# Guess of the experts by bf16 matmuls on upper halves, gate sums on GpSimd: one change to an attention and mixture-of-experts kernel

## The chip, the cores and the metric

The kernel runs on one core of a Trainium2 chip. The metric is the device time of one execution in microseconds. The time before is 491.83 us, the median of three runs (489.59 to 491.87).

## What is computed

Multi-query attention over 8 batches, 16 heads, 384 positions and 64 values a head, and behind it a mixture of experts with a gate in two levels (4 groups of 4 experts). Cut to what matters:

```python
def _attn_ref(q, k, v):                      # q (8,16,384,64), k and v (8,1,384,64)
    scores = np.matmul(q, k.transpose(0, 1, 3, 2)) / np.sqrt(64)
    attn = softmax(scores)
    return np.matmul(attn, v)
x = attn_out.transpose(0, 2, 1, 3).reshape(3072, 1024)
def _moe_ref(x, w_group, w_expert, w1, w2):  # w1, w2: (4,4,1024,1024)
    g_idx = np.argmax(x @ w_group, axis=1)
    for g in range(4):
        xg = x[g_idx == g]
        e_idx = np.argmax(xg @ w_expert[g], axis=1)
        for e in range(4):                   # tokens of xg with e_idx == e
            out[tokens] = gate_weight * (np.maximum(xg_e @ w1[g, e], 0) @ w2[g, e])
```

All tensors are float32. The attention weights are close to even, so a token's `x` is close to the mean of `v` over its batch, and nearly all tokens of a batch choose the same expert.

## The kernel before

**Rounds.** The attention is cut into 192 units (8 batches, 3 row tiles, 8 pairs of heads). The loop at line 1264 takes two units in each of 96 rounds, 12 rounds for each batch. A round has these steps: TensorE (PE) computes the scores of both units into two PSUM buffers `s` (L297, later L283); VectorE (DVE) takes the row maxima (L314); ScalarE (ACT) computes the exponentials with their sums (L319); DVE transposes the probabilities of the round two before into `ring` (L385); DVE takes the reciprocal of the sums (L330); GpSimd (POOL) multiplies by it (`norm`, L334). In some rounds PE multiplies the transposed probabilities with the values (`pv`, L416, 96 matmuls), and ACT copies the result (L427). Queries are transposed on PE (L244) and copied by ACT (L248) in the first five row tiles, later on DVE. Four units of the first batch go another way (`whole`, `pv_whole`, L347, L348, L356).

**Order by hand.** Each engine runs its instructions in the order in which the program writes them. `at(slot, where, fn)` files a step under a round and a place in it, and the loop calls the places in the order "s", "b", then "m0", "m1", "m3" (not in rounds with `pv`), "v", "m2", the first transpose, "t", the second transpose, "w", the norm, "e", "o", "g". So "w" lies ahead of a round's norm on POOL and behind its transposes on DVE, "v" ahead of the transposes, and "e" behind the norm. The norm of rounds 0, 2 and 3 comes one round later (`LATE`). Lines 1202 to 1214 file the steps of the guess.

**The guess.** The kernel has to begin the load of an expert's weights (2 tensors, 1024 x 1024) long before the tokens of a batch are known, so it guesses the expert of each batch from the mean of `v`:

- `guess_load` (L548) takes a weight buffer (`w1`) as scratch, names its parts and loads all rows of `v` into it by three DMAs of SP's queue;
- `guess_fold` (L565, POOL) builds a 128 x 128 matrix of zeros and ones from the identity, which folds the 16 heads of the gate's weights together; it also clears `spread` and makes `sixteen`;
- `guess_gate` (L576, PE) sums the gate weights `wge` (8 chunks of 128 rows, 32 columns) over the heads by eight float32 matmuls with `fold`; ACT copies the result to `gate` (L583);
- `guess_mean` (L585, PE) sums `v` over positions by 12 float32 matmuls with one column; ACT copies `mean` (L594);
- `guess_spread` (L596, POOL) multiplies `gate` by `mean` in two instructions (L600);
- `guess_logits` (L606, PE) sums over the partitions by one float32 matmul (L608); ACT copies `L` (L611);
- `guess_top`, `guess_first` (DVE, L615, L620), `guess_score` (POOL, L628 and L633), `guess_best` (DVE, L639), `guess_pick` (POOL, L644) find the expert of each batch, and `guess_picked` (L652) its mark.

The profile counts each float32 matmul of this kind as two passes. `load_main(0, 0)` reads the pick and issues the first weights on POOL's queue (L746). A matmul on `ident` (`busy`, L129) stands behind `guess_logits`.

**Logits of the first row tile.** `logits(0, 0, 1)` (L449, 16 matmuls) and DVE's copy of its result (`logits_out`, L465) stand in rounds 8 and 9. Their PSUM bank, as those of L244, L347, L356, L416 and all steps of the guess, is one of four that are handed out in turn.

**Main stage and end.** From round 17 on the matmuls of the guessed expert (L799, L784) are put between those of the attention. Tokens whose expert was not guessed are treated at the end; a loop (line 1406) runs once for each batch and expert that is left over.

Of the kernel before, what the change touches and what calls it, by code (L numbers as in the profile page):

```python
# [10 lines left out]
BF16 = mybir.dt.bfloat16  # L11
I32 = mybir.dt.int32
P = 128
# [6 lines left out]
def kernel(  # L20
# [527 lines left out]
    def guess_load():  # L548
# [4 lines left out]
        for name, w in (  # L553
            ("rows", B * ST * D), ("fold", P), ("gate", 32), ("mean", B // 2), ("spread", B * NL), ("L", B * NL),
            ("top", B * NL // 4), ("first", B * NL), ("score", B * GE), ("best", B), ("sixteen", GE),
        ):
            parts[name] = rows[:, at_:at_ + w]
            at_ += w
        for j in range(ST):
            nc.sync.dma_start(  # L560
                out=parts["rows"][:, j * B * D:(j + 1) * B * D].rearrange("p (b d) -> p b d", b=B),
                in_=v[:, 0, j * P:(j + 1) * P, :].rearrange("b p d -> p b d"),
            )

    def guess_fold():  # L565
        g = st["guess"]
        nc.gpsimd.tensor_tensor(
            out=g["fold"].rearrange("p (h d) -> p h d", h=2), in0=ident[:, 0:D].unsqueeze(1).to_broadcast([P, 2, D]),
            in1=ident[:, D:P].unsqueeze(1).to_broadcast([P, 2, D]), op=ALU.add,
        )  # L570
        nc.gpsimd.memset(g["spread"], 0.0)
# [3 lines left out]

    def guess_gate():  # L576
        g, bank = st["guess"], xbank()
        for ko in range(KO):
            nc.tensor.matmul(  # L579
                out=bank[:, 0:32], lhsT=g["fold"], rhs=wge[:, ko, :],  # L580
                start=(ko == 0), stop=(ko == KO - 1),
            )
        nc.scalar.copy(out=g["gate"], in_=bank[:, 0:32])  # L583

    def guess_mean():  # L585
        g, bank = st["guess"], xbank()
        rows = g["rows"].rearrange("p (j i x) -> p j i x", j=ST, x=P)
        for i in range(B // 2):
            for j in range(ST):
                nc.tensor.matmul(  # L590
                    out=bank[:, i:i + 1], lhsT=rows[:, j, i, :], rhs=w4[:, 0, 3:4],
# [4 lines left out]
    def guess_spread():  # L596
        g = st["guess"]
        for h in range(2):
            rows = slice(h * D, (h + 1) * D)
            nc.gpsimd.tensor_tensor(  # L600
                out=g["spread"][rows].rearrange("p (i h e) -> p i h e", h=2, e=NL)[:, :, h, :],
# [4 lines left out]
    def guess_logits():  # L606
        g, bank = st["guess"], xbank()
        nc.tensor.matmul(  # L608
            out=bank[:, 0:B * NL], lhsT=w4[:, 0, 3:4].to_broadcast([P, P]), rhs=g["spread"], start=True, stop=True
# [529 lines left out]
    for b in range(B):  # L1139
# [5 lines left out]
        if early:  # L1145
            at(x, "m2" if edge else "m0", logits, b, 0, 1)
            at(x + edge, "v", logits_out, b, 0, 1)
# [53 lines left out]

    at(3, "g", guess_load)
    at(4, "e", guess_fold)
    at(5, "m3", guess_gate)
    at(8, "m3", guess_mean)
    at(8, "e", guess_spread)
# [3 lines left out]
    at(10, "e", guess_score)  # L1210
    at(11, "v", guess_best)
    at(11, "e", guess_pick)
# [245 lines left out]
```

## Time and profile before

| what | value |
|---|---|
| median of three runs | 491.83 us (489.59, 491.87, 491.83) |
| the profiled execution | 488.88 us |
| its span, first to last instruction | 487.3 us |
| mean granted TensorE clock | 0.988 |
| PE busy | 471.9 us (97%) |
| DVE busy | 402.6 us (83%) |
| ACT busy | 321.0 us (66%) |
| POOL busy | 295.1 us (61%) |

Rows of the timeline hold the start in us, the duration in us, the engine, the line and the operation, the output and inputs by name, their shape, the number of instructions merged into the row and, in brackets, how long the engine stood idle before and what ended that. A row that merges several instructions gives the sum of their time; rows of one engine may overlap a little, since matmuls are pipelined. PEld is the weight load of TensorE. Rows of stretches hold the stretch, its length, the busy time of PE, PEld, DVE, ACT and POOL with the number of instructions, the granted TensorE clock as a share of full speed, the busy share of the DMA engines, and GB/s.

### The profile page before, as it was taken

How to read it: one execution, taken by the hardware profiler on the slowest of the kernel's cores; microseconds unless marked ns; L12 is line 12 of the kernel's file. 1: busy time of each engine (PE TensorE's matmuls, PEld its weight loads, DVE VectorE, ACT ScalarE, POOL GpSimd, SP SyncE). 2: the span in 40 equal slices, each digit the busy share in tenths (PEclk: the TensorE clock that was granted, in tenths of full speed). 3: DMA queues.
4: the chain of work that ended last, by engine and by line, in shares of the span. 5: the costliest groups of instructions: out<-in, count | busy, mean ns of one | idle time of the engine just before them, and what ended most of it. 6: DMA issues, size and time to landing. Idle time of an engine off the chain costs nothing.

```text
span 487.3 us, 21461 instructions
## 1 busy us (share of the span) xinstructions
PE 471.9 (97%) x8935; PEld 284.9 (58%) x8945; DVE 402.6 (83%) x707; ACT 321.0 (66%) x988; POOL 295.1 (61%) x536
## 2 busy tenths in 40 slices
PE   7799898999999999999999999999999999999997
PEld 3366555655665565655666566656665566655554
DVE  4948898998998989898999989898999988883352
ACT  5837675777685866677585767687585867672431
POOL 2836687566656667566656557566757657585223
PEclk9979998999999999999999999999999999999999
DMA  5553079789696969799596968789596947679993
GB/s 135 92 125 77 3 144 239 184 183 193 157 211 180 203 140 191 192 186 205 151 210 176 198 151 179 196 186 207 135 226 176 207 102 145 175 126 212 240 238 144
DMA packets 66291, 83.08 MB, mean 171 GB/s; under 512 B 25447, under 2 KB 42635, under 8 KB 65936
## 3 DMA queue, kind: packets, MB, share of 16 engines
q0 software_dynamic: 18736, 39.32, 44.5%
q1 hardware_dynamic: 46368, 42.03, 32.1%
q8 instruction: 72, 1.18, 0.9%
q10 hardware_dynamic: 1088, 0.33, 0.3%
q14 instruction: 27, 0.22, 0.1%
HBM read 99.94 MB, written 18.22 MB: 242 GB/s over the span
## 4 chain that ended last, share of the span: by engine, by line
PE 89%; DVE 4%; ACT 2%; POOL 2%; issue 1%; DMA 1%; SPq 0%; POOLq 0%; DVEq 0%
PE x L416 24%; PE x L799 22%; PE s L297 17%; PE s L283 7%; PE x L784 7%; PE sb L784 6%; PE x L455 2%; ACT pr L319 2%; DVE ring L385 2%; DVE nmx L314 2%; POOL pr L334 2%; PE x L579 1%; PE x L590 1%; DMA q_sb<-in_q_dram 1%; PE x L1080 0%
## 5 line engine op out<-in xcount | busy, mean ns | idle before, releaser
L334 POOL TENSOR_SCALAR pr<-pr,rinv 128x384 f32<-128x384 f32 x384 | 218.2, 587 | 141.6 <-DVE rinv L330 139.2
L319 ACT ACTIVATE pr<-s,nmx 128x384 f32<-128x384 f32 x384 | 218.4, 579 | 118.2 <-DVE nmx L314 97.3
L314 DVE TENSOR_REDUCE nmx<-s 128x2 f32<-128x768 f32 (+1 forms) x221 | 176.7, 845 | 44.6 <-PE s L297 27.4
L385 DVE STREAM_TRANSPOSE ring<-pr 128x768 f32<-128x768 f32 x189 | 174.7, 953 | 0.0
L416 PE MATMUL x<-ring,v_sb 32*64 32x384 f32 (+3 forms) x3264 | 131.1, 459 | 0.5 <-issue 0.5
L297 PE MATMUL s<-kt,qt 64*64 64x384 f32 x1120 | 107.7, 495 | 5.7 <-ACT pr L319 4.8
L416 PEld LDWEIGHTS x<-ring,v_sb 32*64 32x64 f32 x3264 | 85.3, 132 | 40.8 <-issue 3.4
L319 ACT ACTIVATION_READ_ACCUMULATOR pr<-s,nmx 128x1 f32 x384 | 77.5, 202 | 0.0
L297 PEld LDWEIGHTS s<-kt,qt 64*64 64x64 f32 x1120 | 37.9, 134 | 49.0 <-ACT pr L319 29.7
L799 PE MATMUL x<-xb,w 64*64 64x384 bf16 x1344 | 62.4, 328 | 0.0
L799 PE MATMUL x<-w,h_t 64*64 64x512 bf16 (+1 forms) x1152 | 57.1, 340 | 0.0
L799 PEld LDWEIGHTS <-w 64*64 64x64 bf16 x1344 | 42.6, 108 | 21.0 <-issue 9.6
L799 PEld LDWEIGHTS <-h_t 64*64 64x64 bf16 x1152 | 34.1, 107 | 24.2 <-issue 9.0
L283 PE MATMUL s<-kt,qt 32*64 32x384 f32 x832 | 40.7, 488 | 0.0
L427 ACT COPY xt<-x 128x384 f32<-128x384 f32 (+3 forms) x68 | 26.1, 470 | 12.9 <-PE x L416 12.9
L746 POOL DMA_DIRECT2D w<-in_moe_w_dram x36 | 27.8, 772 | 7.0 <-PE x L416 3.6
L283 PEld LDWEIGHTS s<-kt,qt 32*64 32x64 f32 x832 | 21.4, 131 | 12.2 <-issue 2.7
L826 ACT ACTIVATE h_t<-x 128x384 bf16<-128x384 f32 x56 | 24.5, 498 | 0.2
L784 PEld LDWEIGHTS <-w 128*128 128x128 bf16 x176 | 15.9, 98 | 15.0 <-issue 5.7
L868 ACT ACTIVATE y<-x,gsel 128x512 f32<-128x512 f32 (+1 forms) x43 | 24.5, 639 | 0.0
L784 PEld LDWEIGHTS <-h_t 128*128 128x128 bf16 x152 | 13.8, 97 | 16.0 <-issue 2.5
L784 PE MATMUL x<-xb,w 128*128 128x384 bf16 x112 | 20.6, 327 | 0.0
(176 smaller groups left out, 278.9 us busy)
## 6 DMA issues: line engine op xcount, KB each, us to landing
w<-in_moe_w_dram POOLq DMA_DIRECT2D x36, 1024.0 KB, 11.4
out_dram<-y SPq DMA_DIRECT2D x84, 128.0 KB, 3.3
q_sb<-in_q_dram SPq DMA_DIRECT2D x52, 112.0 KB, 5.8
xb_scratch<-xb SPq DMA_DIRECT2D x7, 768.0 KB, 9.8
q_sb<-in_q_dram SPq DMA_DIRECT2D x24, 224.0 KB, 4.3
q_sb<-in_q_dram SPq DMA_DIRECT2D x52, 64.0 KB, 8.7
v_sb<-in_v_dram SPq DMA_DIRECT2D x32, 96.0 KB, 3.3
kk<-in_k_dram SPq DMA_DIRECT2D x28, 92.0 KB, 3.1
```

The costliest lines, as they stand in the source:

```text
L283: last = nc.tensor.matmul(out=st["s", us[g // 2]][m * D:(m + 1) * D, g % 2, 0:S], lhsT=q4[r, (g + n) % 2, ts(m, D)], rhs=kt[r, :], start=( ...
L297: nc.tensor.matmul(out=s[m * D:(m + 1) * D, h, 0:S], lhsT=qt[r, ts(2 * cc + m, D)], rhs=kt[r, :], start=True, stop=True, tile_position=(h ...
L314: top = nc.vector.tensor_reduce(out=nmx[:, hs], in_=s[:, hs, 0:S], axis=AX.X, op=ALU.max, negate=True)
L319: ex = nc.scalar.activation(out=pr[:, h, :], in_=s[:, h, 0:S], func=ACTF.Exp, bias=nmx[:, h:h + 1], scale=1.0, accum_out=ssum[:, k, h:h + 1],)
L334: nc.gpsimd.tensor_scalar(out=pr, in0=pr, scalar1=rinv[:, k, h:h + 1], scalar2=1.0, op0=ALU.mult, op1=ALU.mult)
L385: nc.vector.transpose(out=ring[:, slot(u) // 4, slot(u) % 4].rearrange("p h s -> p (h s)"), in_=st.pop(("pr", u))[:].rearrange("p h s -> p ...
L416: at_last = nc.tensor.matmul(out=to, lhsT=v_sb[rows, turned(n, h), :], rhs=probs, start=(n == 0), stop=(n == NB - 1), tile_position=(32 * ...
L427: nc.scalar.copy(out=flat[:, first:first + nc_, ts(i, 32)], in_=o[:, 0:32 * nc_].rearrange("p (c q) -> p c q", c=nc_))
L746: behind(nc.gpsimd.dma_start(out=w[:, o:o + wide, :], in_=views[n][ds(e, 1), :, o:o + wide, :].rearrange("o p c f -> (o p) c f")), wait)
L784: nc.tensor.matmul(out=view(bank), lhsT=weights(k), rhs=moving(k), start=(k == 0), stop=(k == KO - 1))
L799: last = nc.tensor.matmul(out=view(banks[r ^ part][c * D:(c + 1) * D, :]), lhsT=weights(k)[rows, c * D:(c + 1) * D], rhs=moving(k)[rows], ...
L826: nc.scalar.activation(out=h_t[:, fc, :], in_=hp[:, 0:S], func=ACTF.Relu)
```

## The change

The values that the guess multiplies are read or written as bf16, in the upper half of each float32 word (`high`), so that its matmuls take one pass. `fold` and `spread` are written that way, the rows of `v` are read that way, and the column of ones is the bf16 tile `ones`. The gate's eight chunks are no longer summed by eight matmuls: POOL adds them in three instructions (`guess_heads`), and one matmul folds the result. The scratch is named in a step of its own (`guess_place`), so that `fold`, the cleared `spread` and `sixteen` are made in round 0. `guess_gate` moves from round 5 to round 8, behind `guess_mean`; `guess_heads` stands in round 7, behind the norm. `guess_score`, `guess_best` and `guess_pick` move to the place "w". `logits` of the first row tile moves from round 8 to round 12, its copy from round 9 to 13.

```diff
-    def guess_load():
+    def guess_place():
...
-            ("rows", B * ST * D), ("fold", P), ("gate", 32), ("mean", B // 2), ("spread", B * NL), ("L", B * NL),
+            ("rows", B * ST * D), ("fold", P), ("gate", 32), ("part", 128), ("heads", 32), ("mean", B // 2), ("spread", B * NL), ("L", B * NL),
...
+    def guess_load():
+        parts = st["guess"]
         for j in range(ST):
             nc.sync.dma_start(
...
+    def high(x):
+        return x.bitcast(BF16).rearrange("p (x two) -> p x two", two=2)[:, :, 1]
+
     def guess_fold():
+        guess_place()
...
-            out=g["fold"].rearrange("p (h d) -> p h d", h=2), in0=ident[:, 0:D].unsqueeze(1).to_broadcast([P, 2, D]),
+            out=high(g["fold"]).rearrange("p (h d) -> p h d", h=2), in0=ident[:, 0:D].unsqueeze(1).to_broadcast([P, 2, D]),
...
-        nc.gpsimd.memset(g["spread"], 0.0)
+        nc.gpsimd.memset(high(g["spread"]), 0.0)
...
+    def guess_heads():
+        g = st["guess"]
+        part = g["part"].rearrange("p (k e) -> p k e", e=32)
+        nc.gpsimd.tensor_tensor(out=part, in0=wge[:, 0:4, :], in1=wge[:, 4:8, :], op=ALU.add)
+        nc.gpsimd.tensor_tensor(out=part[:, 0:2, :], in0=part[:, 0:2, :], in1=part[:, 2:4, :], op=ALU.add)
+        nc.gpsimd.tensor_tensor(out=high(g["heads"]), in0=part[:, 0, :], in1=part[:, 1, :], op=ALU.add)
+
     def guess_gate():
         g, bank = st["guess"], xbank()
-        for ko in range(KO):
-            nc.tensor.matmul(
-                out=bank[:, 0:32], lhsT=g["fold"], rhs=wge[:, ko, :],
-                start=(ko == 0), stop=(ko == KO - 1),
-            )
+        nc.tensor.matmul(out=bank[:, 0:32], lhsT=high(g["fold"]), rhs=high(g["heads"]), start=True, stop=True)
...
-                    out=bank[:, i:i + 1], lhsT=rows[:, j, i, :], rhs=w4[:, 0, 3:4],
+                    out=bank[:, i:i + 1], lhsT=high(rows[:, j, i, :]), rhs=ones[:, 0:1],
...
-                out=g["spread"][rows].rearrange("p (i h e) -> p i h e", h=2, e=NL)[:, :, h, :],
+                out=high(g["spread"])[rows].rearrange("p (i h e) -> p i h e", h=2, e=NL)[:, :, h, :],
...
-            out=bank[:, 0:B * NL], lhsT=w4[:, 0, 3:4].to_broadcast([P, P]), rhs=g["spread"], start=True, stop=True
+            out=bank[:, 0:B * NL], lhsT=ones[:], rhs=high(g["spread"]), start=True, stop=True
...
         if early:
+            x = s0 + (12 if edge else 10)
             at(x, "m2" if edge else "m0", logits, b, 0, 1)
...
+    at(0, "g", guess_fold)
     at(3, "g", guess_load)
-    at(4, "e", guess_fold)
-    at(5, "m3", guess_gate)
+    at(7, "e", guess_heads)
     at(8, "m3", guess_mean)
+    at(8, "m3", guess_gate)
...
-    at(10, "e", guess_score)
-    at(11, "v", guess_best)
-    at(11, "e", guess_pick)
+    at(10, "w", guess_score)
+    at(11, "w", guess_best)
+    at(11, "w", guess_pick)
```

In the changed program the lines of these steps lie up to twelve further down: L592 is the matmul of `guess_gate`, L600 that of `guess_mean`, L618 that of `guess_logits`, and L586 to L588 are the three sums.

The first place is PE's row of instructions at the end of round 5: the scores (L297), a transpose of queries (L244), L356 of a whole unit, and the scores of round 6.

```order
 L297 MATMUL s<-kt,qt 64x384 x8
 L244 MATMUL x<-ident,q_sb 128x128 x4
-L579 MATMUL x<-wge,rows 128x32 x8
 L356 MATMUL x<-ring,grem_all 64x128 x6
 L297 MATMUL s<-kt,qt 64x384 x8
```

The eight matmuls of the gate sums are gone there, and nothing stands in their place.

The second place is PE in rounds 8 and 9; `rows` is the scratch of the guess. Before:

```order
L244 MATMUL x<-ident,q_sb 128x128 x4
L590 MATMUL x<-w_108,rows 128x1 x12
L449 MATMUL x<-wge,xt 64x32 x16
L297 MATMUL s<-kt,qt 64x384 x8
L244 MATMUL x<-ident,q_sb 128x128 x4
L608 MATMUL x<-rows,w_108 128x160
L129 MATMUL x<-ident 128x512
```

And now, from the last of the twelve pairs of the mean on:

```order
L600 LDWEIGHTS rows
L600 MATMUL x<-ones,rows 128x1
L592 LDWEIGHTS rows
L592 MATMUL x<-rows 128x32
L297 MATMUL s<-kt,qt 64x384 x8
L244 MATMUL x<-ident,q_sb 128x128 x4
L618 LDWEIGHTS ones
L618 MATMUL x<-rows,ones 128x160
L129 MATMUL x<-ident 128x512
```

L449 has left, and L592 stands between the mean and the scores of round 9.

The third place is POOL from the norms of rounds 5 to 7 (or 2 to 7) on; L437 are casts of the first row tile, L334 the norms, four instructions a round. Before:

```order
L334 TENSOR_SCALAR pr<-pr,rinv 128x384 x12
L437 CAST xb<-xt 128x2x128
L437 CAST xb<-xt 128x512
L437 CAST xb<-xt 128x2x128
L334 TENSOR_SCALAR pr<-pr,rinv 128x384 x4
L600 TENSOR_TENSOR rows<-rows 64x4x20 x2
L334 TENSOR_SCALAR pr<-pr,rinv 128x384 x8
L628 TENSOR_TENSOR rows<-rows 128x128
L633 TENSOR_TENSOR rows<-rows 128x128
L334 TENSOR_SCALAR pr<-pr,rinv 128x384 x4
L644 TENSOR_SCALAR picks<-rows 128x8
```

And now:

```order
L334 TENSOR_SCALAR pr<-pr,rinv 128x384 x24
L586 TENSOR_TENSOR rows<-wge 128x128
L587 TENSOR_TENSOR rows<-rows 128x64
L588 TENSOR_TENSOR rows<-rows 128x32
L437 CAST xb<-xt 128x2x128
L437 CAST xb<-xt 128x512
L437 CAST xb<-xt 128x2x128
L334 TENSOR_SCALAR pr<-pr,rinv 128x384 x4
L610 TENSOR_TENSOR rows<-rows 64x4x20 x2
L334 TENSOR_SCALAR pr<-pr,rinv 128x384 x4
L638 TENSOR_TENSOR rows<-rows 128x128
L643 TENSOR_TENSOR rows<-rows 128x128
```

Three sums stand between the norm of round 7 and the casts, and the product of round 10 (L638, L643) stands ahead of that round's norm.

## The prediction

> **What bounds the kernel now.** I read the page first, then the stretches by granted clock, then the timeline of the first 70 us, where all touched instructions lie. Away from the start TensorE alone sets the pace; the second row of the next fence shows it busy 119.90 of 120 us, so what a change saves in the first 85 us moves everything behind it by as much. The other rows are stretches of 3.41 us (length, busy time of PE, PEld, DVE, ACT, POOL, then clock, DMA share, GB/s).
>
> ```profile
> PEclk9979998999999999999999999999999999999999
> ```
> ```profile
> 120.00:240.00 120.00, 119.90 (x2470) 73.10 (x2460) 109.22 (x174) 83.81 (x261) 75.51 (x131) 1.00 0.80 179
> ```
> ```profile
> 21.90:25.32 3.42, 1.46 (x12) 0.63 (x12) 3.42 (x6) 2.50 (x9) 2.87 (x7) 0.99 0.76 67
> 25.32:28.73 3.41, 3.20 (x16) 3.23 (x16) 0.64 (x2) 0.90 (x3) 2.58 (x6) 0.50 0.93 210
> 28.73:32.14 3.41, 3.41 (x26) 2.20 (x30) 0.00 (x0) 0.56 (x2) 0.00 (x0) 0.51 0.66 153
> ...
> 56.04:59.45 3.41, 2.57 (x44) 1.01 (x28) 3.20 (x7) 2.31 (x10) 1.19 (x3) 1.00 0.02 5
> ...
> 76.52:79.93 3.41, 1.43 (x32) 0.80 (x24) 2.12 (x5) 1.71 (x5) 2.91 (x5) 0.99 1.10 261
> 79.93:83.34 3.41, 3.41 (x41) 2.53 (x37) 3.41 (x6) 2.52 (x9) 0.80 (x2) 0.51 1.12 231
> ```
>
> Twice PE was busy only 1.43 to 1.46 us of such a stretch, and the clock of the next was 0.50; stretches with 2.57 us and more kept 1.00. All edges lie on one grid of 3.41 us.
>
> I call the work on two units a round; round i starts with DVE's first maximum (L314). In rounds 1 to 5 DVE is busy without a break; then comes the hole that the change aims at:
>
> ```profile
> 10.58 4.53 POOL L334 TENSOR_SCALAR pr<-pr,rinv 128x384 f32<-128x384 f32 x8 [8.68 <-DVE rinv L330]
> ...
> 22.85 0.66 PE L244 MATMUL x<-ident,q_sb 128*128 128x128 f32 x4
> ...
> 24.78 0.46 POOL L567 TENSOR_TENSOR rows<-ident 128x128 f32<-128x128 f32 x1
> ...
> 25.07 0.59 ACT L319 ACTIVATE pr<-s,nmx 128x384 f32<-128x384 f32 x1
> 25.48 0.21 POOL L572 TENSOR_SCALAR rows<-tie 128x16 f32<-128x16 f32 x1
> 25.53 3.60 PE L579 MATMUL x<-wge,rows 128*128 128x32 f32 x16 [2.02 <-POOL rows L567]
> 25.62 0.60 ACT L248 COPY qt<-x 128x512 f32<-128x512 f32 x1
> 25.82 0.14 DVE L330 RECIPROCAL rinv<-ssum 128x4 f32<-128x4 f32 x1
> 29.05 1.55 PE L356 MATMUL x<-ring,grem_all 128*64 128x128 f32 x12
> 30.53 2.26 PE L297 MATMUL s<-kt,qt 64*64 64x384 f32 x16
> 30.65 0.37 ACT L362 COPY xt<-x 128x256 f32<-128x256 f32 x1 [1.30 <-PE x L356]
> 32.16 1.82 DVE L314 TENSOR_REDUCE nmx<-s 128x2 f32<-128x768 f32 x2 [6.20 <-PE s L297]
> 32.72 2.21 PE L416 MATMUL x<-ring,v_sb 32*64 32x192 f32 x96
> ```
>
> PE waits 2.02 us for the fold, spends 3.60 us on the gate sums, partly at half clock, and only then reaches the scores of round 6: DVE stands 6.20 us.
>
> **Round 6: what goes.** Without L579, PE does L356 right after L244 (23.5 to 24.4), and the scores when ACT has freed the two banks, the second at 25.07 + 0.59 = 25.66. DVE is free at 25.82 + 0.14 = 25.96 and finds the first unit ready. Round 6 starts at 25.96 in place of 32.16: 6.2 us gained. The sums over values that follow (L416) now wait for ACT's copy L362, 25.62 + 0.60 + 0.37 = 26.6, 0.65 after the round's start where it was 0.56, and DVE's own work fills the rounds; I give 0.3 back over rounds 6 and 7. Round 8 then starts at 33.6: **5.9 us gained**. The fold, its memset and the sixteen (0.9 us in all) move into POOL's 8.68 us of idleness at the start and cost nothing; the mean's rows are loaded at the same place of SP's queue.
>
> **Rounds 8 and 9: what comes.**
>
> ```profile
> 39.51 1.82 DVE L314 TENSOR_REDUCE nmx<-s 128x2 f32<-128x768 f32 x2
> 39.52 2.27 POOL L334 TENSOR_SCALAR pr<-pr,rinv 128x384 f32<-128x384 f32 x4 [1.36 <-DVE rinv L330]
> ...
> 40.56 2.74 PE L590 MATMUL x<-w,rows 128*128 128x1 f32 x24
> ...
> 41.73 1.31 POOL L437 CAST xb<-xt 128x256 bf16<-128x256 f32 x3
> ...
> 43.23 1.12 PE L449 MATMUL x<-wge,xt 128*64 128x32 f32 x32
> ...
> 44.28 1.52 PE L297 MATMUL s<-kt,qt 64*64 64x384 f32 x16
> ...
> 45.23 1.82 DVE L314 TENSOR_REDUCE nmx<-s 128x2 f32<-128x768 f32 x2 [2.10 <-PE s L297]
> 45.46 0.71 POOL L600 TENSOR_TENSOR rows<-rows 64x80 f32<-64x80 f32 x2
> ...
> 46.60 1.02 PE L129 MATMUL x<-ident 128*128 128x512 f32 x2
> ...
> 48.87 1.79 DVE L314 TENSOR_REDUCE nmx<-s 128x2 f32<-128x768 f32 x2
> ...
> 55.25 0.42 POOL L628 TENSOR_TENSOR rows<-rows 128x128 f32<-128x128 f32 x1
> ```
>
> Before, round 9 came 5.72 us after round 8 (45.23 - 39.51), since L590 and L449 stood ahead of its scores. L590's 24 passes of 0.114 us become 12 of no more than that (1.4 us), L449 leaves. But L592 now waits for POOL, and the scores of round 9 are queued behind L592. From the start of round 8, POOL does the norm (2.27), then the three new sums: 128 elements 0.42 (L628), 64 elements about 0.33 (near L600's 0.355), 32 about 0.25 (between that and L572's 0.21), with gaps 1.2 us. They end at 3.5. Then L592, one pass (0.1 to 0.2), and the scores; 0.95 us after these begin (44.28 to 45.23) DVE starts round 9, at 4.7: 1.0 better than before, and DVE's own work (1.82 + 1.83 of transposes + 0.14) would have taken 3.8. The shorter mean is hidden in this wait.
>
> On POOL the casts (1.31) and the norm of round 8 (2.27) follow, then the spread (0.71): it ends 8.0 after the start of round 8 (41.6), where it was 46.17 - 39.51 = 6.7. PE reaches L618, which needs the spread, when scores and L244 are done, at 39.4, and stands idle until 41.65: **a new wait of 2.2 us**. Behind it in PE's queue stand the filler L129 (1.02) and the scores of round 10, for which DVE waits. L618 has no row; between one pass (0.1) and L608's two of before (0.5) I take 0.15. Round 10 starts at 41.65 + 0.15 + 1.0 + 0.95 = 43.75 in place of 48.87: **5.1 us gained**, less than at round 8.
>
> **Rounds 11 to 13.**
>
> ```profile
> 53.22 1.82 DVE L314 TENSOR_REDUCE nmx<-s 128x2 f32<-128x768 f32 x2 [0.29 <-PE s L297]
> ...
> 56.25 0.29 DVE L639 TENSOR_REDUCE rows<-rows 128x8 f32<-128x128 f32 x1 [1.21 <-POOL rows L633]
> ...
> 58.26 1.85 DVE L314 TENSOR_REDUCE nmx<-s 128x1 f32<-128x384 f32 x3
> ...
> 62.18 1.89 DVE L314 TENSOR_REDUCE nmx<-s 128x1 f32<-128x384 f32 x3
> ...
> 63.27 0.88 PE L356 MATMUL x<-ring,grem_all 128*64 128x128 f32 x12
> ```
> ```profile
> 78.72 1.77 PE L297 MATMUL s<-kt,qt 64*64 64x384 f32 x16 [1.98 <-ACT pr L319]
> ...
> 80.18 2.86 PE L799 MATMUL x<-xb,w 64*64 64x384 bf16 x32
> ```
>
> In round 11 DVE stood 1.21 us at L639 with two transposes queued behind. The product now goes ahead of the norm of round 10, the maximum behind the transposes; PE's scores then bind and the round lasts 4.25 in place of 5.04: 0.8 gained. L449 (1.12) goes into round 12 where PE waits for POOL anyway, free. But its bank is freed by DVE's copy in round 13, behind 1.89 us of maxima, and L356 takes that bank: it begins 2.15 after the round's start where it was 63.27 - 62.18 = 1.09; some of this is slack, 0.65 is lost. Sum: 5.1 + 0.8 - 0.65 = **5.25**. The first weights are asked for about 0.4 us sooner in their round; L799 follows its scores at 80.18 without a wait, so that is worth nothing.
>
> **The clock.** The new wait, 39.4 to 41.65, lies inside one cell of the grid (38.90 to 42.32): PE would be busy 1.2 us of 3.41, less than in both cells that were followed by 0.50. The next cell then runs at half clock, and there (scores, sums over values) PE binds: 3.41 / 2 = 1.7 lost. 5.25 - 1.7 = **3.5 us**.
>
> The Trainium skill speaks against this term: the page "TensorE: Matmul & The Clock Gate", section "HAM oscillation — how this bites in real kernels", has the clock fall for idle gaps over about 3.4 us only; by that rule the sum would stay 5.25, but the trace has the clock at 0.50 after a gap of 2.02 us, and I go by the trace.
>
> The profiled execution took 488.88 us around a span of 487.3; 488.88 - 3.5 = 485.4. The median of the three runs is 491.83, 2.95 above; the same on top gives **488.3**. A measurement of this kernel can tell about 0.5% (2.5 us) from no change.
>
> **Rivals.**
> A: the wait comes, the clock does not fall, because the grid lies otherwise or the wait is shorter. 491.83 - 5.25 = 486.6. For it: where the cells lie hangs on 3.41 us of luck; a wait of 2.2 us fits wholly into one in a third of the positions and mostly in some two thirds. Against it: 2 of 2 such waits in the trace.
> B: besides that, the second low stretch (79.93) falls away, as its wait of 1.98 us is moved against the grid: 1.7 more, 484.9.
> C: the low clock at 25 to 32 us is not in the run that gives the median of before. At full clock L579 takes 16 x 0.114 = 1.8 (not 3.60), L356 0.88 (not 1.55), the scores 1.52 (not 2.26): 3.2 of the gain was not there. 5.25 - 3.2 = 2.0, so 489.8, and 491.5 if the new wait lowers the clock. The three runs of before differ by 2.3 us, which speaks for it. The same page, section "What's actually happening", has these windows free-running against the kernel's start; one trace cannot show that.
> D, slower: POOL's chain becomes the bound. It decides if the three sums with their 4-byte steps in bf16 take over 1.2 + 3.5 = 4.7 us; at 2.4 us each (7.2) the time is 494.3. Rows of POOL on 64 to 128 elements, 0.36 to 0.46, speak against it.
> E, the change does not do what it says: cutting the lower halves changes a pick, and the loop at the end runs for that batch. It loads its weights with nothing to cover them, at least 11.4 us (row below): over 503. Worked out from the drawn inputs, the closest lead, of two experts in batch 7, is -0.234 against -0.294, with cut halves -0.221 against -0.281: no pick changes.
>
> ```profile
> w<-in_moe_w_dram POOLq DMA_DIRECT2D x36, 1024.0 KB, 11.4
> ```
>
> **How the numbers follow.** Forecast (wait and low clock) 0.45, A 0.27, B 0.10, C 0.14, D 0.03, E 0.01. Of the forecast's 0.45 I put 0.08 within 0.5%, since 3.5 lies 1.0 above that bound. Faster 0.37 + 0.27 + 0.10 = 0.74; same 0.08 + 0.14 = 0.22; slower 0.04. The range reaches from just under B to just over C's 489.8: 484.5 to 490.2; it leaves out D, E, C's 491.5 and the tails.
>
> **What would show it.** In the changed profile DVE's round 6 should start near 26.0 and round 8 near 33.6; L592 should wait under 1.5 us for POOL, L618 about 2.2; L639's successor should wait for nothing; L356 of round 13 should wait for DVE; the clock should be 0.50 in one cell after 41 us and 1.00 from 25 to 32. I am wrong if round 6 still starts after 28 (something else held the scores), if L618 waits under 1 us, or if rounds 14 to 17 give the gain back.

## The result and the profile after

The changed kernel took 483.35 us, the median of four executions (482.81 to 485.16), against 491.32 for the kernel before (four, 489.59 to 491.87): a ratio of 0.985 with a 95% interval of 0.9812 to 0.9888. The profiled execution took 482.9 us around a span of 481.3, with a mean granted clock of 0.996 (before: 488.88, 487.3 and 0.988). The change is faster, as forecast, but by 8.0 us (1.5%) where 3.5 were forecast; the result lies 4.95 us under the predicted 488.3 and below the range.

First the clock row of the page, then two stretches of the granted clock's grid in the changed profile (columns as in the prediction: length, busy time of PE, PEld, DVE, ACT, POOL, clock, DMA share, GB/s):

```profile
PEclk9998999999999999999999999999999999999999
```
```profile
34.57:37.98 3.41, 1.42 (x25) 0.86 (x17) 3.34 (x5) 3.06 (x11) 3.25 (x8) 0.99 0.33 76
37.98:41.39 3.41, 3.41 (x20) 1.40 (x20) 1.42 (x2) 1.04 (x6) 3.41 (x8) 0.51 0.77 191
```

Two low slices of before (the third and the seventh of the page) are one now, the fourth, and it lies between 37.98 and 41.39, not behind 41.39 as forecast. Next the timeline of the changed kernel, the rows that answer to those of before:

```profile
23.39 1.79 DVE L314 TENSOR_REDUCE nmx<-s 128x2 f32<-128x768 f32 x2
...
24.46 0.88 PE L356 MATMUL x<-ring,grem_all 128*64 128x128 f32 x12
...
25.69 0.88 PE L297 MATMUL s<-kt,qt 64*64 64x384 f32 x8 [0.35 <-ACT pr L319]
...
26.90 1.82 DVE L314 TENSOR_REDUCE nmx<-s 128x2 f32<-128x768 f32 x2
...
34.29 1.82 DVE L314 TENSOR_REDUCE nmx<-s 128x2 f32<-128x768 f32 x2
...
35.47 0.44 PE L600 MATMUL x<-ones,rows 128*128 128x1 bf16 x12
...
36.66 0.46 POOL L586 TENSOR_TENSOR rows<-wge 128x128 f32<-128x128 f32 x1
...
37.20 0.32 POOL L587 TENSOR_TENSOR rows<-rows 128x64 f32<-128x64 f32 x1
...
37.59 0.26 POOL L588 TENSOR_TENSOR rows<-rows 128x32 bf16<-128x32 f32 x1
...
37.90 0.19 PE L592 MATMUL x<-rows 128*128 128x32 bf16 x1 [1.99 <-DVE ring L385]
...
39.65 0.96 DVE L314 TENSOR_REDUCE nmx<-s 128x2 f32<-128x768 f32 x1 [1.73 <-PE s L297]
...
41.31 0.71 POOL L610 TENSOR_TENSOR rows<-rows 64x80 bf16<-64x80 f32 x2
...
42.08 0.23 PE L618 MATMUL x<-rows,ones 128*128 128x160 bf16 x1 [0.39 <-POOL rows L610]
...
44.08 1.82 DVE L314 TENSOR_REDUCE nmx<-s 128x2 f32<-128x768 f32 x2 [0.39 <-PE s L297]
...
52.53 1.89 DVE L314 TENSOR_REDUCE nmx<-s 128x1 f32<-128x384 f32 x3 [0.41 <-PE s L297]
...
55.23 0.80 DVE L662 TENSOR_TENSOR ohs_all<-rows 128x128 f32<-128x128 f32 x1
...
57.53 0.88 PE L356 MATMUL x<-ring,grem_all 128*64 128x128 f32 x12
...
60.15 1.83 DVE L314 TENSOR_REDUCE nmx<-s 128x2 f32<-128x768 f32 x2
...
69.78 1.89 DVE L314 TENSOR_REDUCE nmx<-s 128x1 f32<-128x384 f32 x3 [1.27 <-PE s L297]
...
73.52 1.79 DVE L314 TENSOR_REDUCE nmx<-s 128x2 f32<-128x768 f32 x2
```

At the top L356 and the scores of round 6 (25.69) have nothing ahead of them but a third of a us for ACT; the rows from 34.29 to 44.08 are rounds 8 to 10 with the three sums, those behind them rounds 12 to 17. The row of L592 names DVE's transposes (L385), which ended within 0.01 us of POOL's last sum; that the wait is for the sums is shown by the run with the sums early, below, where it is gone. And of the kernel before, the starts of rounds 5, 14, 16 and 17, which the prediction did not show:

```profile
22.36 0.92 DVE L314 TENSOR_REDUCE nmx<-s 128x2 f32<-128x768 f32 x1
...
65.47 1.83 DVE L314 TENSOR_REDUCE nmx<-s 128x2 f32<-128x768 f32 x2
...
74.54 1.89 DVE L314 TENSOR_REDUCE nmx<-s 128x1 f32<-128x384 f32 x3 [0.71 <-PE s L297]
...
79.65 1.83 DVE L314 TENSOR_REDUCE nmx<-s 128x2 f32<-128x768 f32 x2 [1.29 <-PE s L297]
```

The rows of L314 are the starts of the rounds, so the two profiles can be laid side by side (us; "gain" is the first line less the second):

| start of round | 5 | 6 | 8 | 9 | 10 | 12 | 14 | 16 | 17 | span |
|---|---|---|---|---|---|---|---|---|---|---|
| before | 22.36 | 32.16 | 39.51 | 45.23 | 48.87 | 58.26 | 65.47 | 74.54 | 79.65 | 487.3 |
| changed | 23.39 | 26.90 | 34.29 | 39.65 | 44.08 | 52.53 | 60.15 | 69.78 | 73.52 | 481.3 |
| gain | -1.03 | 5.26 | 5.22 | 5.58 | 4.79 | 5.73 | 5.32 | 4.76 | 6.13 | 6.0 |

Rounds 5 to 6 take 6.29 us less (5.26 + 1.03). Round 5 itself began 1.03 later; over the fourteen profiles of this study its start ranges from 22.15 to 23.39, and a second profile of the changed kernel has 22.65, so this part belongs to the execution and not to the change. From round 17 on the two run alike: 6.13 there, 6.0 at the end.

### The profile page after: what moved, and what is told of

It is laid out like the page before. It is cut to its first block, busy times and chain, and to the rows that moved or that the text cites. A ratio compares the mean times of both kernels' runs of the same rounds, so it can differ in the third digit from the quotient of the medians.

```text
span 481.3 us, 21407 instructions
## 1 busy us (share of the span) xinstructions
PE 466.4 (97%) x8907; PEld 277.4 (58%) x8917; DVE 402.8 (84%) x707; ACT 320.8 (67%) x988; POOL 296.3 (62%) x539
## 4 chain that ended last, share of the span: by engine, by line
PE 88%; DVE 5%; ACT 3%; POOL 1%; issue 1%; DMA 1%; SPq 0%; DVEq 0%; ACTq 0%
PE x L416 25%; PE x L809 22%; PE s L297 17%; PE s L283 8%; PE x L794 7%; PE sb L794 6%; ACT pr L319 3%; DVE nmx L314 3%; PE x L455 2%; DVE ring L385 1%; POOL pr L334 1%; PE x L129 1%; DMA q_sb<-in_q_dram 1%; PE x L1090 0%; PE x L992 0%
## 5 line engine op out<-in xcount | busy, mean ns | idle before, releaser
L334 POOL TENSOR_SCALAR pr<-pr,rinv 128x384 f32<-128x384 f32 x384 | 218.2, 586 | 133.7 <-DVE rinv L330 131.3
L314 DVE TENSOR_REDUCE nmx<-s 128x2 f32<-128x768 f32 (+1 forms) x221 | 176.8, 845 | 39.7 <-PE s L297 22.2
L385 DVE STREAM_TRANSPOSE ring<-pr 128x768 f32<-128x768 f32 x189 | 174.8, 954 | 0.0
L297 PE MATMUL s<-kt,qt 64*64 64x384 f32 x1120 | 109.1, 499 | 5.7 <-ACT pr L319 5.0
L297 PEld LDWEIGHTS s<-kt,qt 64*64 64x64 f32 x1120 | 37.3, 134 | 53.0 <-ACT pr L319 33.5
L809 PE MATMUL x<-xb,w 64*64 64x384 bf16 x1344 | 60.9, 323 | 0.0
L809 PEld LDWEIGHTS <-w 64*64 64x64 bf16 x1344 | 40.9, 107 | 21.4 <-issue 10.1
```

What stands on the lines that cost most here:

```text
L297: nc.tensor.matmul(out=s[m * D:(m + 1) * D, h, 0:S], lhsT=qt[r, ts(2 * cc + m, D)], rhs=kt[r, :], start=True, stop=True, tile_position=(h ...
L314: top = nc.vector.tensor_reduce(out=nmx[:, hs], in_=s[:, hs, 0:S], axis=AX.X, op=ALU.max, negate=True)
L334: nc.gpsimd.tensor_scalar(out=pr, in0=pr, scalar1=rinv[:, k, h:h + 1], scalar2=1.0, op0=ALU.mult, op1=ALU.mult)
L385: nc.vector.transpose(out=ring[:, slot(u) // 4, slot(u) % 4].rearrange("p h s -> p (h s)"), in_=st.pop(("pr", u))[:].rearrange("p h s -> p ...
L809: last = nc.tensor.matmul(out=view(banks[r ^ part][c * D:(c + 1) * D, :]), lhsT=weights(k)[rows, c * D:(c + 1) * D], rhs=moving(k)[rows], ...
```

## The experiments

In the experiments "the theory" was at first that of the prediction, with the wait for the fold at its head; what fell is said where it fell. "Rk" is the start of round k.

**Both kernels once more.** The kernel before, as it is:

> The kernel before, unchanged, for a second profile. Places are counted from the start of round 5 (R5). Theory 'grid': the low clock falls on a free grid of 3.41 us, so the stretch of half clock behind the 2.0 us wait in round 5 need not come again; with it round 6 starts 9.8 us after R5 as in the first profile, without it at about 6.9 (L579 1.8 in place of 3.6, L356 0.9 in place of 1.55). Theory 'program': it is tied to the kernel's start and comes again at 25 to 32 us. The wait of TensorE ahead of the scores of round 17 (1.98 us) comes again at the same instruction if it is the loading of code, whose edge lies at a fixed instruction; it is gone if it was luck of the DMA queues.

Measured: 491.38 us (489.16 to 493.08, ten executions) against 491.99, ratio 0.9996 (0.9971 to 1.0021); R5 to R6 10.20 us, and the wait ahead of the scores of round 17 was 1.95 us again. What the prediction read in one profile of before is there in the second. The low clock came again too, from 25.23 to 32.06; that it is not tied to the kernel's start is seen in two further runs on the kernel before, where it began at 26.16 (fold first) and 27.63 (gate weights first). The changed kernel, as it is:

> The changed kernel, unchanged, for a second profile and more times. Places are counted from the start of round 5. Theory 'loading' (the 1.95 us wait ahead of round 17's scores in the kernel before is the loading of code at the edge behind TensorE's row 2178, which the changed program meets later in its work): round 17 again starts 3.7 to 4.0 us after round 16, in place of 5.1. Theory 'luck': 5.1 may come back. Round 6 3.5, round 10 20.7 or, without a low clock, about 19.5 to 20.7.

Measured: 482.08 us (481.74 to 482.55) against 491.24, ratio 0.981 (0.9777 to 0.9843). R8 to R9 took 5.33 us and R8 to R10 9.76 (5.36 and 9.79 in the first profile), and R16 to R17 took 3.74 again: the gain and its shape recur.

**What held round 6: three runs on the kernel before.** First the fold alone:

```diff
+    at(0, "g", guess_fold)
...
-    at(4, "e", guess_fold)
```

> The kernel before, with the fold matrix, the cleared spread and the sixteen made in round 0 and nothing else changed. Theory 'stall' (the gain is the hole in round 5, most of it the wait for the fold and the low clock behind it): TensorE does L579's sixteen passes right after the queries' transpose, in 1.8 us, so round 6 starts 4.6 us after R5 in place of 9.8; round 8 follows 7.4 later; rounds 8 to 10 as before (9.4). About 5 us faster than before. Rival 'narrow' (the gain is the fewer passes of bf16 matmuls): round 6 gains only the 2.0 us of the wait, and the kernel is about 2 us faster at most.

Measured: 491.82 us, ratio 0.999 (0.9956 to 1.0024). Nothing was gained, and the row shows why:

```profile
25.63 3.12 PE L583 MATMUL x<-wge,rows 128*128 128x32 f32 x16 [2.08 <-issue]
```

The fold had been ready since the start of the kernel, and the gate sums (L583 here) still waited 2.08 us, for something that the profile does not name. Beside the fold they read only the gate weights `wge`. Next the fold as it was and the load of these weights ahead of the load of `v`:

```diff
+    at(0, "g", load_gate)
     at(0, "g", load_v, 0)
-    at(0, "g", load_gate)
```

> The kernel before with one line moved: the load of the gate weights is asked for ahead of the load of the values, the matrix fold stays where it was. With fold made first and this load first the time was 485.4 us; with fold made first alone nothing was gained. Theory (the fold was the second of two things that came at nearly the same time, ending at about 25.3 us where the gate weights came at about 25.5): the wait ahead of the gate sums stays at 1.5 us or more, round 6 starts 6 to 10 us after round 5, and the time is 488 to 491 us. Rival (the gate weights alone held the sums): round 6 starts about 4.5 us after round 5 and the time is about 485.4 us.

Measured: 491.56 us, ratio 1.0004 (0.997 to 1.0038).

```profile
25.42 0.46 POOL L567 TENSOR_TENSOR rows<-ident 128x128 f32<-128x128 f32 x1
...
25.93 2.10 PE L579 MATMUL x<-wge,rows 128*128 128x32 f32 x16 [1.78 <-POOL rows L567]
```

Now it is the fold that is late, and R5 to R6 takes 8.06 us. Then both edits together:

> The kernel before with two edits: fold, spread and sixteen made in round 0, and the five loads of the gate's weights put ahead of the four loads of v on SP's queue. Theory 'loads' (L579 waited for the last of these loads, which is issued at 22.2 and takes 3.1 us, and not for the fold): L579 starts right behind the queries' transpose, runs at full clock in 1.8 us, and round 6 starts 4.6 to 5.2 us after R5 in place of 9.8; round 9 as before 5.7 after round 8; in all 4 to 5 us faster than before. Rival: something else holds L579, it starts at 25.6 again, and the time is that of before.

Measured: 485.42 us (485.12 to 488.93), ratio 0.9899 (0.9848 to 0.995).

```profile
23.06 1.79 DVE L314 TENSOR_REDUCE nmx<-s 128x2 f32<-128x768 f32 x2
...
24.05 1.87 PE L583 MATMUL x<-wge,rows 128*128 128x32 f32 x16
...
27.60 1.82 DVE L314 TENSOR_REDUCE nmx<-s 128x2 f32<-128x768 f32 x2 [0.94 <-PE s L297]
```

No wait, full clock (1.87 us where it was 3.60), and R5 to R6 takes 4.54 us, where before had 9.80 and the changed kernel has 3.51. So two things came late at nearly the same time, with only one of them early the other still holds the sums, and with both early the sixteen passes that the change takes off TensorE cost only 1.03 us there. Most of the gain of the change (5.8 of 9.2 us by the medians on this chip, 491.24 to 485.42 and to 482.08) can be had with the old float32 sums in their old place.

**The narrowing.** The changed kernel with float32 values in all matmuls of the guess:

```diff
-    out=bank[:, i:i + 1], lhsT=high(rows[:, j, i, :]), rhs=ones[:, 0:1],
+    out=bank[:, i:i + 1], lhsT=rows[:, j, i, :], rhs=w4[:, 0, 3:4],
```

(and the same for the fold, the heads, `spread` and the logits)

> The changed kernel with all its moves and the three sums on GpSimd, but float32 values in the guess's matmuls (two passes each, 12 float32 matmuls for the mean). Theory 'stall': within 1 us of the changed kernel, since the mean's 2.7 us end 0.3 us before or after the sums that L592 waits for; round 6 3.5 us after R5, round 10 about 20.7 to 21.2. Rival 'narrow': most of the gain is lost, the kernel is 4 us or more slower than the changed one.

Measured: 483.12 us (481.94 to 484.47), ratio 0.9803 (0.9775 to 0.9831): within 1.1 us of the changed kernel's two medians (483.35, 482.08).

```profile
34.94 3.02 PE L600 MATMUL x<-w,rows 128*128 128x1 f32 x24
...
37.06 0.25 POOL L588 TENSOR_TENSOR rows<-rows 128x32 f32<-128x32 f32 x1
```

The mean takes 3.02 us where bf16 takes 0.44, but it ends at 37.96 and POOL's last sum at 37.31: most of it lies where TensorE would wait for POOL. In this profile the clock was low for 6.8 us behind it and R10 came 11.45 us after R8 (9.79 in the changed kernel), so the float32 form is not free; by the medians it costs at most about 1 us. In the title's words the bf16 matmuls are the change; on the chip they are at most a small part of its gain.

**POOL's chain and the clock.** The changed kernel with the three sums two rounds sooner:

```diff
-    at(7, "e", guess_heads)
+    at(5, "e", guess_heads)
```

> The changed kernel with the three sums behind the norm of round 5 in place of round 7, where GpSimd stands idle for 1.2 us a round. Theory 'chain' (in rounds 7 to 9 GpSimd's chain norm, sums, casts, norm, spread sets when round 10 starts, and the low clock in the changed profile lies under it): L592 waits for nothing, round 9 starts 3.8 to 4.3 us after round 8 (5.36 in the changed profile), round 10 9.0 to 9.3 after round 8 (9.79). 0.5 to 0.8 us faster than the changed kernel. Rival 'clock' (the low clock, not the chain, set round 10 in the changed profile): 1.3 to 1.7 us faster if no low clock falls there, nothing gained if one does.

Measured: 482.09 us (480.04 to 482.85), ratio 0.9781 (0.9757 to 0.9805). L592 waited for nothing and R8 to R9 took 3.55 us, but R8 to R10 took 10.33, later than in the changed kernel (9.79), so the rival's second case came: a low clock fell there, and nothing was gained:

```profile
37.07:40.48 3.41, 1.49 (x13) 0.72 (x14) 3.41 (x6) 2.87 (x12) 3.17 (x7) 0.99 0.81 205
40.48:43.89 3.41, 3.41 (x15) 1.12 (x18) 0.42 (x2) 0.85 (x4) 2.27 (x4) 0.51 0.02 5
```
```profile
40.45 0.29 PE L618 MATMUL x<-rows,ones 128*128 128x160 bf16 x1 [1.79 <-POOL rows L610]
...
40.54 1.99 PE L129 MATMUL x<-ident 128*128 128x512 f32 x2
...
42.46 2.17 PE L297 MATMUL s<-kt,qt 64*64 64x384 f32 x16
```

The wait of 1.79 us in front of L618 brought the low clock behind it, where TensorE's work is what DVE waits for: the filler took 1.99 us (1.06 in the changed kernel) and the scores 2.17 (1.52), 1.58 us more together. This is the prediction's clock term (1.7) at the place where the prediction put it. The single executions of this run say the same: the two with a clock of 0.999 or more took 480.04 and 481.31 us, the four with 0.996 took 481.67 to 482.85. So it was also tried to take away this second wait, by the spread ahead of POOL's norm:

```diff
-    at(7, "e", guess_heads)
+    at(5, "e", guess_heads)
...
-    at(8, "e", guess_spread)
+    at(8, "w", guess_spread)
```

> The changed kernel with the three sums behind the norm of round 5 and the spread ahead of the norm of round 8, so that the spread ends about 4.4 us after the start of round 8 in place of 7.8. Theory 'chain': neither L592 nor L618 waits, no stretch of half clock follows, and round 10 starts 7.6 to 8.2 us after round 8 (9.8 in the changed kernel, 10.3 with the sums early alone): 1.6 to 2.2 us faster than the changed kernel. Rival 'queue' (the filler L129 and the scores set the pace): 9.0 or more.

Measured: 480.23 us (479.41 to 480.61), ratio 0.9769 (0.9736 to 0.9802), the fastest of all, 1.85 us under the changed kernel beside it on the same chip (482.08).

```profile
38.01 0.72 POOL L610 TENSOR_TENSOR rows<-rows 64x80 bf16<-64x80 f32 x2 [0.47 <-ACT rows L593]
...
38.78 0.23 PE L618 MATMUL x<-rows,ones 128*128 128x160 bf16 x1
...
40.98 1.80 DVE L314 TENSOR_REDUCE nmx<-s 128x2 f32<-128x768 f32 x2
```

L618 waits for nothing, R10 comes at 40.98, 7.10 after R8 (33.88), and the clock is nowhere at half before 478 us. The norm, which now stands behind the spread, is not missed.

**The logits of the first row tile** in their old rounds 8 and 9:

```diff
-            x = s0 + (12 if edge else 10)
```

> The changed kernel with L449 and its copy back in rounds 8 and 9. Theory 'chain' (GpSimd's chain sets round 10): L449's 1.1 us lie under the wait for the spread, round 10 stays 19.5 to 20.7 us after R5, and round 13 gets its bank at once, so rounds 12 to 14 take 7.2 in place of 7.6: 0.4 us faster or the same. Rival 'queue' (what stands ahead of round 9's scores on TensorE counts): 1.1 us slower at round 10.

Measured: 483.58 us (482.08 to 484.04), 1.5 us over the changed kernel beside it on the same chip (482.08); ratio 0.9835 (0.979 to 0.988). L449 stands again behind L592 and ahead of the scores of round 9, and R8 to R9 takes 7.18 us in place of 5.33. R10 comes 10.95 after R8, 1.2 later than in the changed kernel, as the rival has it; at round 17 0.74 of this is left. Moving the logits is worth 0.7 us by the profiles and 1.5 by the medians.

**Round 17.** Three runs on what removed the wait of 1.98 us ahead of its scores. The product, the maximum and the pick at their old places:

```diff
-    at(10, "w", guess_score)
-    at(11, "w", guess_best)
-    at(11, "w", guess_pick)
+    at(10, "e", guess_score)
+    at(11, "v", guess_best)
+    at(11, "e", guess_pick)
```

> The changed kernel with the product, the maximum and the pick of the guess filed at their old places (behind the norm of round 10, ahead of the transposes of round 11, behind the norm of round 11). Theory: VectorE stands again about 1.2 us in round 11 for the product, rounds 10 to 12 take about 9.3 us in place of 8.45, and the first weights are asked for later; the time is 0.5 to 1.0 us longer. Rival (what is late there is made up before the main stage, since TensorE waits less in rounds 14 to 17): rounds 10 to 12 are longer but round 17 starts at the same distance from round 5 as in the changed kernel, and the time is the same to 0.3 us.

Measured: 482.55 us (482.01 to 483.54), ratio 0.983 (0.9799 to 0.9861). R10 to R12 took 9.40 us, as the theory has it, but R17 came 50.16 us after R5 (50.13 in the changed kernel), as the rival has it: the 0.95 us are made up. (Between the medians, taken on two chips, lie 0.5 us.) Then 28 more pairs of weight load and matmul at the start of the changed kernel; the filler behind them is halved, from 512 columns to 256, so that the start takes no longer:

```diff
-    busy(ones)
-    filled = busy(ident)
+    start = busy(ones)
+    for _ in range(28):
+        nc.tensor.matmul(out=start[:, 0:1], lhsT=ones[:], rhs=ones[:, 0:1], start=True, stop=True)
+    filled = busy(ident, 2)
```

> The changed kernel with 28 more pairs of a weight load and a matmul of one column on TensorE at the very start, where it waits for the queries anyway; nothing else is altered. In the three profiles with the old guess TensorE stood 1.5 to 1.95 us ahead of the scores of round 17, each time at the same count of TensorE instructions from the start; the changed kernel issues 28 pairs fewer ahead of that place, and the stop was not seen there. Theory (the stop hangs on the count of instructions, as the fetch of a block of code would): with 28 pairs more the stop is back ahead of the scores of round 17, 1.5 to 2 us long; rounds 16 to 17 take 5.1 to 5.6 us in place of 3.74, and the time is 1 to 2 us longer than the changed kernel's. Rival (the stop came from the guess itself, the clock or a transfer): rounds 16 to 17 stay at 3.74 and the time within 0.5 us of the changed kernel's.

Measured: 483.02 us (481.26 to 484.46), ratio 0.9823 (0.9779 to 0.9866); R16 to R17 stayed at 3.74 us. The theory as it stood, a stop of fixed length at a fixed count, fell. What this profile lost, it lost elsewhere: R8 to R10 took 11.43 us in place of 9.79, since the clock was low from 38.62 to 45.44, also behind L618, and the filler and the scores of round 10 ran at half clock:

```profile
41.79 1.99 PE L129 MATMUL x<-ident 128*128 128x512 f32 x2
...
43.71 2.35 PE L297 MATMUL s<-kt,qt 64*64 64x384 f32 x16
```

There is more to see of the stop. Counting TensorE's records in order of time (matmuls, weight loads and the waits of its sequencer), all fourteen profiles have a stop of 0.3 to 1.2 us at record 1985, and it stayed at 1985 here, though the 28 pairs had moved other work to that count. Record 2241, 256 further, is where before stood 1.88 us (1.98 up to the next matmul); in this run the DMA engines had a pause when TensorE came to it, and with the old picks they had none. So both edits were put together:

> The changed kernel with both edits at once: the product, the maximum and the pick of the guess at their old places, and 28 more pairs of weight load and matmul on TensorE at the start. In all profiles TensorE stops at record 1985 of its stream, and 256 records later once more, for up to 1.9 us, where the DMA engines are full then (share 1.10 to 1.13); with 28 pairs alone the DMA engines had a pause there (0.33) and no stop was seen; with the picks at their old places alone the DMA engines were full and the stop, at record 2241, lasted 0.50 us. Theory (a stop at a fixed count, whose length is set by how full the DMA engines are and how fast TensorE has got there): with both edits the stop at record 2241 falls among the short matmuls ahead of the scores of round 17 again, with the DMA engines full, and lasts 1.2 to 1.9 us; rounds 16 to 17 take 4.8 to 5.6 us in place of 3.74, and the time is 0.7 to 1.5 us longer than with either edit alone (about 484). Rival (the stop belonged to the old guess): rounds 16 to 17 take 3.74 and the time is that of the two alone, 482.6 to 483.0.

Measured: 485.35 us (483.37 to 486.35), ratio 0.9875 (0.9847 to 0.9903), 2.3 us and more over either edit alone, more than was expected. The stretches in which TensorE reaches record 2241, in the run with 28 pairs, in that with the old picks and in that with both:

```profile
72.00:74.00 2.00, 2.00 (x76) 1.47 (x76) 2.00 (x3) 1.86 (x7) 2.00 (x3) 1.00 0.33 91
```
```profile
72.00:74.00 2.00, 1.36 (x20) 0.70 (x21) 2.00 (x5) 0.93 (x3) 1.42 (x4) 1.00 1.09 256
```
```profile
72.00:74.00 2.00, 1.42 (x65) 0.92 (x59) 2.00 (x3) 1.91 (x8) 1.99 (x3) 1.00 1.13 259
```

And the rows of the stop itself, with the old picks and with both edits:

```profile
74.01 1.31 PE L809 MATMUL x<-xb,w 64*64 64x384 bf16 x20 [0.50 <-issue]
```
```profile
75.27 1.20 PE L297 MATMUL s<-kt,qt 64*64 64x384 f32 x12 [1.85 <-issue]
```

| | pairs ahead | picks | lowest DMA share in the 4 us before | stop at record 2241 | R16 to R17 |
|---|---|---|---|---|---|
| before | old | old | 1.12 | 1.88 | 5.11 |
| changed | 28 fewer | new | 0.47 | none | 3.74 |
| 28 pairs | old | new | 0.33 | none | 3.74 |
| old picks | 28 fewer | old | 1.09 | 0.50 | 3.74 |
| both | old | old | 1.13 | 1.85 | 5.44 |

The stop is back with both edits, at the size that it had before. It was seen only with full DMA engines, and cost most where TensorE came to it over many short matmuls. All six profiles with the old picks and the old count of pairs have R16 to R17 at 4.66 to 5.44, all eight others at 3.74 or 3.75. So either part of the change is enough to keep the stop off round 17: the picks made sooner, so that the DMA engines have their pause by then, or the 28 pairs less. Of the 2.86 us that this run takes longer from R5 to its end than the one with the old picks alone, the stop is 1.70 (5.44 - 3.74); another 1.47 lie ahead of R16, with a stretch at low clock from 42.3 to 45.7 behind L618's wait, and 0.3 are made up behind R17.

## Why the prediction was wrong

By its steps, in its order (a small one first: in round 1 DVE did wait, 0.84 us, so it was without a break from round 2 on only):

- *"PE waits 2.02 us for the fold"*: half of it. The fold and the gate weights were late together; either alone gained nothing (ratios 0.999 and 1.0004), both together 0.9899. The change does away with both, since its sums read the weights only at 36.66, so the size was not touched by this error.
- *Round 6, 6.2 us*: right. R5 to R6 is 6.29 us shorter. *Round 8, 5.9*: 6.25 without the start of round 5.
- *Rounds 8 to 10*: right in mechanism. POOL's sums took 0.46, 0.32 and 0.26, with gaps 1.19 (forecast 1.2); L592 waited 1.99 (forecast: under 1.5), since the mean ahead of it, bounded at 1.4 us, took 0.44. Round 9 was forecast 4.7 after R8; it came at 5.36, and at 4.65 in the run with the old picks, whose clock did not fall. The spread ended 7.73 after R8 (forecast 8.0), R10 came 9.79 after R8 (forecast 10.15). L618 waited 0.39 where 2.2 were forecast, because the low clock brought TensorE there late; with the old picks it waited 1.95.
- *Round 13, 0.65 lost to L356*: wrong place, near size. L356 began at 57.53, 0.63 after its round, and waited for nothing. Rounds 12 to 14 lost 0.41 all the same; there L662, the mark of the pick, takes 0.80 us of DVE, where the same row of before took 0.25; with the old picks the rounds lost nothing (7.20 against 7.21).
- *Sum 5.25*: the profiled pair has 5.32 at round 14, low clock and all, with the late start of round 5 in it, and 6.35 without. So the agreement of 5.32 with 5.25 is luck: from round 5 on the sum was 1.1 too small, 0.35 up to round 8, 0.37 up to round 10, 0.14 up to round 12 and 0.24 behind it.
- **The failed step: "The next cell then runs at half clock, and there (scores, sums over values) PE binds: 3.41 / 2 = 1.7 lost."** A low stretch came, but one wait sooner, behind L592, and so beneath POOL's chain, which lasted until 42.02 whatever TensorE did: with no low stretch at all (the run with the old picks) R10 came 9.76 after R8, with it 9.79. The prediction had looked for a low stretch behind L618's wait alone; L592's wait, made longer by the short mean, was nearly as long. Where the low stretch does fall behind L618 (the run with the sums early) it costs 1.58. So the mechanism exists and its size was right, but it does not come every time. Of the five profiles whose rounds 8 to 10 are those of the changed kernel, three have R10 9.76 to 9.79 after R8, the run with 28 pairs 11.43 and that with both edits 10.67. The term was a matter of where the grid lies, and was put on the likeliest path as if it were sure. By the prediction's own sign (L618 waits under 1 us) it was wrong.
- *"L799 follows its scores at 80.18 without a wait, so that is worth nothing"*: failed. The first weights asked for sooner, and the 28 pairs less, each removed the stop ahead of round 17. R16 to R17 gained 1.37 us; 0.56 were lost at the stop before it, at record 1985 (1.01 us where before had 0.45), which is the fall of the gain from 5.32 to 4.76 in the table.
- **The second failed step: "The median of the three runs is 491.83, 2.95 above; the same on top gives 488.3."** The changed median lies 0.45 above its profiled execution, not 2.95. This is half the miss (2.5 of 4.95 us); the other half is 1.7 of the clock term, 0.1 of the sum up to round 14 and 0.7 of rounds 14 to the end.

Why the offset went is in the clocks of the single executions. All 72 of the kernel before that stand beside these runs:

| granted clock of the execution | executions | median us |
|---|---|---|
| 0.992 to 0.993 | 10 | 489.1 |
| 0.988 to 0.990 | 17 | 489.9 |
| 0.985 to 0.986 | 24 | 491.6 |
| 0.978 to 0.983 | 21 | 493.1 |

A straight line through them gives 0.35 us for each us at half clock, and 486.6 us for a clock that is never low. The median clock of 0.986 is 13.7 us at half clock (2 x 0.014 x 490), 4.8 us by this line. The changed kernel's ten executions have 0.996 to 1.000, at most 3.9 us. At most 1.4 us are left of that (0.35 x 3.9). So by this line 3.4 us or more of the gain is that the clock falls less often, and the rest is waits and work that are gone; the prediction let the change add a low stretch, whereas it takes away the waits behind which most of them came. The run with fold and gate weights early, where the wait for the sums alone is gone, has 0.996 or more in three of four executions, which fits; how much of the 0.35 is the clock itself and how much goes with it was not separated. Rival C (the low clock of before was luck of one profile) had the same reading upside down: 0.988 was one of the better executions.

Of the rivals, A and B come nearest: no clock term, and the wait at round 17 gone; B's 484.9 lacks what the offset hid. D and E did not come near.

## What to carry to other kernels

A wait with one releaser named may have two that came together: before costing its removal, ask what else the instruction reads and when that landed. Around waits of about 2 us on TensorE, count what the clock does as a chance over executions, for the kernel before as much as for the changed one, and do not add the distance between one profile and the median to the other kernel. When a chain of small steps crosses several engines, look for what stands ahead of each step on its queue: here two lines filed sooner gave a fifth as much again as the whole change (1.85 on 9.2 us).

## What was not expected of the hardware

- **The clock fell behind stretches of its grid in which TensorE was busy for about half of the time or less.** Waits of 1.98 and 1.95 us (L592, L618) in the run with the old picks left it at 1.00, since each straddled an edge:

```profile
32.85:36.26 3.41, 2.12 (x32) 1.07 (x25) 3.41 (x6) 3.05 (x13) 2.70 (x6) 1.00 0.23 50
36.26:39.68 3.42, 2.21 (x21) 1.00 (x21) 2.40 (x4) 1.76 (x8) 3.34 (x8) 1.00 0.95 233
39.68:43.09 3.41, 1.98 (x15) 0.81 (x18) 1.94 (x4) 2.39 (x9) 2.60 (x7) 1.00 0.05 14
```

Of the stretches quoted here, 1.98 us busy and more kept the clock, 1.42 and 1.49 lost it. Over all fourteen profiles fifteen stretches of 1.28 to 1.77 us busy had half clock behind them, but two of 1.53 (both edits) and 1.60 (gate weights first) had not, so no one bound on the busy time parts them. Nor is a short busy time needed: with the float32 mean the profile has TensorE busy without a break, and the next stretch was low all the same:

```profile
33.89:37.30 3.41, 3.41 (x34) 2.86 (x26) 3.41 (x5) 3.05 (x12) 3.25 (x8) 0.99 0.29 67
37.30:40.71 3.41, 3.41 (x22) 1.79 (x21) 0.81 (x3) 0.69 (x3) 3.41 (x8) 0.50 0.78 200
```

Most of that stretch (34.94 to 37.30) are passes with a single column; the run with the fold first has a second such stretch (39.81 to 43.22, busy throughout, 0.50 behind it), and the float32 mean lies in it too. Whether these passes count as work for the clock was not tried. The Trainium skill, page "TensorE: Matmul & The Clock Gate", section "What's actually happening", has the windows free-running against the kernel's start; the traces agree (edges at about 36.2 in the run with the old picks, at about 34.5 and 37.9 in the changed kernel). The rule of idle gaps over about 3.4 us, which the Trainium skill has on the same page under "HAM oscillation — how this bites in real kernels" and which the prediction weighed, does not hold here: gaps of 1.79 and 1.99 us were enough.
- **TensorE stopped at two fixed counts of its records**, 1985 and 2241, 256 apart, for up to 1.88 us, where the DMA engines were full (share 1.09 and more by the table). Full engines are not enough: at records 2497 and 3521, one block and five blocks of 256 on, the share was 1.09 to 1.15 in all fourteen profiles, and none has a stop. There TensorE had taken 6.3 to 8.3 us for the 256 records before; ahead of the stops it had taken 4.4 to 4.8, the stop not counted, and 6.1 ahead of that of 0.50. The page of the changed kernel has a queue for instructions:

```profile
q8 instruction: 71, 1.16, 1.0%
```

71 packets for 18,078 records are one for 255. The Trainium skill, page "Runtime: NRT & Kernel Launch", section "Instruction fetch mechanics", says that instructions are fetched in blocks of 256 by a DMA queue of the engine's own, mostly hidden. The counts agree; that it stays hidden did not hold here. That the fetch is what TensorE waits for is argued from the counts, not shown.
